# A scan's decays from cumulated rows, blocks of one chunk of all batches, and engine orders written by hand, in a kernel of SSD scan and hardswish MLP

## The chip, the cores and the metric

The kernel runs on one core of one Trainium2 chip. The metric is the device time of one execution in microseconds (us); the median of three runs is given. The core has TensorE (PE; its weight loads are listed apart as PEld), VectorE (DVE), ScalarE (ACT), GpSimd (POOL) and SyncE (SP), each with an instruction queue of its own, and 16 DMA engines. Transfers are issued here from SP's and ACT's queues.

## The reference

Two parts follow each other. The first is a scan (Mamba2 SSD) over 4 batches, 8 heads, 768 tokens, with 32 channels and 16 state rows per head; the second is an MLP with a hardswish between its two products, over 3072 tokens of 256 channels and 2048 inner channels.

```python
log_a = np.log(np.clip(a, 1e-06, 1.0))
for c in range(nc):                      # chunks of the sequence
    cum = np.cumsum(la, axis=-1)
    L = np.exp(cum[:, :, :, None] - cum[:, :, None, :]) * causal
    y_intra = einsum('bhij,bhjd->bhid', einsum('bhin,bhjn->bhij', Cc, Bc) * L, xc)
    y_inter = einsum('bhin,bhnd->bhid', Cc, state) * np.exp(cum)[:, :, :, None]
    y[:, :, sl] = y_intra + y_inter
    decay_from_j = np.exp(cum[:, :, -1:] - cum)
    state = exp(sum(la)) * state + sum_j(Bc * xc * decay_from_j)
x = y.transpose(0, 2, 1, 3).reshape(B * S, H * D)
h = x @ w_in
out = (h * np.clip(h + 3.0, 0.0, 6.0) / 6.0) @ w_out
```

The weights come as float64 and are made float32 on the chip; all products are float32. Both kernels take chunks of 128 tokens, which give the same sums as the reference's chunks of 32.

## The kernel before

`ssd(g)` does one chunk of one batch, so there are 24 of them. Decays between tokens come from PE: POOL spreads log a into `lu` (line 234), PE multiplies it by a triangle (`after`, line 242) and gets the sums of log a over (j, i] for all pairs of tokens, two heads at a time, in the first half of the PSUM tile `lg`. Beside it, in the other half, stands the product C.B of the same two heads (line 245), which uses 32 of PE's 128 rows. ACT takes the exponential (249), POOL sets what lies above the diagonal to zero (250), DVE multiplies the two halves into `M` (253). There are three `lg` buffers for the four pairs of heads. Then PE adds what the state gives (259) and the chunk's own part (265) in `y`, and the new state's product (275), and DVE scales and adds the state (278, 282). The chunk's C, B and scaled C are turned by PE (223).

A block of the MLP has 512 tokens: four chunks of one batch, or of two neighbouring ones. `mlp_in(k, f)` computes 128 of the 2048 inner channels (two matmuls, 295), ACT and DVE make the hardswish (299, 300: tiles `r` and `gT`); `mlp_out(k, t)` sums 16 matmuls for 128 tokens (306), ACT copies (310), SP stores (312). A weight piece (16 of them, 512 KB each) is loaded on ACT's queue (94) into one of three `raw` buffers and decoded by `decode_w` (110 to 126: five steps on DVE, three on POOL). The first block's four `ssd` and the eight pieces of `w_in` come ahead of the first `mlp_in`; the pieces of `w_out` and the next block's `ssd` are placed between the `mlp_in` and `mlp_out` of each block.

The order of instructions on each engine is made by the tile framework's scheduler, which ranks them by priority; it isn't the order of the program text. It sets the waits between engines too.

Of the kernel before, what the change touches and what calls it, by code (L numbers as in the profile page):

```python
# [12 lines left out]
PSUM = bass.MemoryType.PSUM  # L13


@with_exitstack
def kernel(
# [23 lines left out]
    NC = S // P                 # chunks in a sequence  # L41
    T = NB * S
    TB = 512                    # tokens in a block of the MLP
    NBLK = T // TB
    CPB = TB // P               # chunks in a block
# [4 lines left out]
    assert NH * N == P and NH * D == DM == 2 * P and D == 32 and 2 * N == 32  # L50
    assert DF == NF * P == 8 * PC and NC * P == S and NBLK * TB == T

    const = ctx.enter_context(tc.tile_pool(name="const", bufs=1))
    loads = ctx.enter_context(tc.tile_pool(name="loads", bufs=5))
    att = ctx.enter_context(tc.tile_pool(name="att", bufs=2))
    ffn = ctx.enter_context(tc.tile_pool(name="ffn", bufs=2))
    ps_l = ctx.enter_context(tc.tile_pool(name="ps_l", bufs=3, space=PSUM))
    ps_m = ctx.enter_context(tc.tile_pool(name="ps_m", bufs=1, space=PSUM))
    ps_y = ctx.enter_context(tc.tile_pool(name="ps_y", bufs=1, space=PSUM))
    ps_f = ctx.enter_context(tc.tile_pool(name="ps_f", bufs=3, space=PSUM))  # L60

# [1 line left out]
    moe_w_in, moe_w_out = moe_w_in.bitcast(U32), moe_w_out.bitcast(U32)  # L63
    a_sb = const.tile([NB * NH, S], FP32, name="a_sb")
# [4 lines left out]
    def load(g):  # L69
        b, c = divmod(g, NC)  # L70
        sl = slice(c * P, (c + 1) * P)
        bc = loads.tile([P, 2, NH, N], FP32, name="bc")
        xt = loads.tile([P, NH, D], FP32, name="xt")
        for j, src in enumerate((B, C)):
            nc.sync.dma_start(out=bc[:, j], in_=src[b, :, sl, :].rearrange("h s n -> s h n"))
        nc.sync.dma_start(out=xt, in_=x[b, :, sl, :].rearrange("h s d -> s h d"))
        loaded[g] = bc, xt

    for g in range(CPB):
        load(g)  # L80
# [3 lines left out]
    NP = 8                      # pieces of each weight matrix  # L84
    raws = {}

    def load_w(i):
        raw = loads.tile([P, 2, 2 * PC], U32, name="raw", bufs=3)
# [5 lines left out]
        nc.scalar.dma_start(out=raw, in_=src)  # L94
        raws[i] = raw

    def decode_w(i):
        """float64 words to float32: (1 + mantissa) * (sign, 2 ** exponent)."""
        words = raws.pop(i).rearrange("p k (f w) -> p k f w", w=2)
# [5 lines left out]
        e = att.tile([P, 2, PC], U32, name="we")  # L105
        m = att.tile([P, 2, PC], U32, name="wm")
        t = att.tile([P, 2, PC], FP32, name="wt")
        # the exponent, its bias changed from 1023 to 127, at float32's place;
        # what is too small for float32 becomes 0, what is too large infinite
        nc.vector.tensor_scalar(  # L110
# [16 lines left out]
        if i + 3 < 2 * NP:  # L127
            load_w(i + 3)

    for i in range(3):  # L130
        load_w(i)
# [67 lines left out]
    def ssd(g):  # L199
# [72 lines left out]
        if c == NC - 1:  # L272
            return
# [86 lines left out]
```

## Time and profile before

| | us |
|---|---|
| median of three runs | 551.46 |
| lowest and highest | 550.2 and 551.74 |
| span of the profiled execution | 548.1 |
| PE busy in it (90%) | 492.0 |
| DVE, POOL, ACT busy | 217.2, 125.3, 117.7 |
| matmuls of `mlp_in` (L295), busy | 174.4 |
| matmuls of `mlp_out` (L306), busy | 171.5 |
| matmuls of the decay sums (L242), busy | 59.0 |
| matmuls of the scores (L245), busy | 37.1 |

The profile is that of one execution; its times start with the span. Busy time of an engine is the union of its instructions; L242 is line 242 of the kernel. A group's line gives, after the bar, its busy time and the mean duration of one instruction, then the idle time of the engine ahead of these instructions and what ended most of it. Matmuls are pipelined and their ends are modelled, so what one costs in a row is read from start to start. In a row of a stretch, the numbers after the stretch and its length are the busy times of PE, PEld, DVE, ACT and POOL with their counts, then the granted clock of PE, the share of the DMA engines and GB/s.

### The profile page before, as it was taken

Reading aid. Unit: us, or ns where it says so; the run is one execution under the profiler, and the core shown is the slowest. Engines: PE = TensorE matmul, PEld = TensorE weight load, DVE = VectorE, ACT = ScalarE, POOL = GpSimd, SP = SyncE. Lnnn points to the kernel's source line nnn. Section 1 sums busy time; section 2 is a strip of 40 time slices with the busy share of each in tenths; the row PEclk is TensorE's granted clock in tenths of the full one; section 3 lists DMA queues with packets and bytes.
Section 4 is the critical chain, followed back from the end, with each engine's and each line's share of the span. In section 5 each row is a group of like instructions: output and inputs, shape, how many; then the busy total and the mean of one; then the engine's idle time right before and its main releaser. Section 6 shows DMA issues by size and latency. Waiting matters only on the chain.

```text
span 548.1 us, 5534 instructions
## 1 busy us (share of the span) xinstructions
PE 492.0 (90%) x2120; PEld 306.9 (56%) x2120; DVE 217.2 (40%) x404; ACT 117.7 (21%) x246; POOL 125.3 (23%) x178
## 2 busy tenths in 40 slices
PE   1697788899999898899898898999898999999997
PEld 1353333366754476663466664456674457774586
DVE  5978989732125522115522215422205452104300
ACT  1211033121032321122321122321112421114300
POOL 6574765612101202202202202012202021100000
PEclk9999899899999999999999999999999999999999
DMA  8834242111010101101101101101000000000000
GB/s 174 168 97 77 86 126 86 12 27 29 20 19 11 18 15 20 32 16 19 11 10 30 29 20 19 10 11 29 11 19 2 0 2 10 11 19 0 1 19 19
DMA packets 82761, 18.27 MB, mean 33 GB/s; under 512 B 75536, under 2 KB 78608, under 8 KB 82736
## 3 DMA queue, kind: packets, MB, share of 16 engines
q1 hardware_dynamic: 78384, 9.54, 11.7%
q10 hardware_dynamic: 4352, 8.39, 4.6%
q8 instruction: 16, 0.26, 0.2%
q14 instruction: 9, 0.07, 0.0%
HBM read 14.78 MB, written 3.15 MB: 33 GB/s over the span
## 4 chain that ended last, share of the span: by engine, by line
PE 69%; DVE 14%; POOL 10%; issue 4%; ACT 2%; DMA 1%; ACTq 0%; DVEq 0%
PE f L306 30%; PE f L295 25%; PE lg L242 6%; DVE M L253 4%; PE lg L245 4%; POOL L L250 3%; POOL lu L234 3%; DVE state L282 2%; PE y L265 2%; ACT L L249 2%; POOL we L113 2%; DVE we L117 1%; DMA raw<-in_moe_w_in_dram 1%; POOL we L115 1%; POOL wt L122 1%
## 5 line engine op out<-in xcount | busy, mean ns | idle before, releaser
L295 PE MATMUL f<-yT,w_in 128*128 128x512 f32 x384 | 174.4, 604 | 0.0
L306 PE MATMUL f<-w_out,gT 128*128 128x256 f32 x768 | 171.5, 381 | 0.0
L306 PEld LDWEIGHTS f<-w_out,gT 128*128 128x128 f32 x768 | 144.8, 190 | 24.4 <-issue 5.6
L300 DVE SCALAR_TENSOR_TENSOR gT<-r,f 128x512 f32<-128x512 f32 x96 | 65.8, 685 | 147.8 <-ACT r L299 147.1
L295 PEld LDWEIGHTS f<-yT,w_in 128*128 128x128 f32 x384 | 72.0, 192 | 82.9 <-issue 81.9
L250 POOL TENSOR_SCALAR_AFFINE_SELECT L<-L 128x256 f32<-128x256 f32 x96 | 40.7, 443 | 312.3 <-ACT L L249 311.9
L299 ACT ACTIVATE r<-f,half 128x512 f32<-128x512 f32 x96 | 66.0, 687 | 132.6 <-PE f L295 120.4
L242 PE MATMUL lg<-lu,after 128*128 128x256 f32 x192 | 59.0, 424 | 20.0 <-DVE M L253 17.2
L253 DVE TENSOR_TENSOR M<-L,lg 128x256 f32<-128x256 f32 x96 | 38.1, 418 | 67.7 <-POOL L L250 67.7
L242 PEld LDWEIGHTS lg<-lu,after 128*128 128x128 f32 x192 | 34.2, 202 | 34.4 <-DVE M L253 26.2
L249 ACT ACTIVATE L<-lg 128x256 f32<-128x256 f32 x96 | 32.0, 384 | 95.8 <-PE lg L245 92.9
L234 POOL TENSOR_TENSOR lu<-upto,la 128x1024 f32<-128x1024 f32 x24 | 47.2, 1968 | 10.0 <-PE lg L242 9.6
L310 ACT COPY ob<-f 128x256 f32<-128x256 f32 x24 | 8.9, 372 | 176.2 <-PE f L306 176.2
L265 PE MATMUL y<-M,xt 128*32 128x128 f32 x384 | 28.8, 292 | 16.3 <-DVE M L253 16.3
L245 PE MATMUL lg<-cT,bcT 32*128 32x256 f32 x192 | 37.1, 456 | 3.4 <-DVE cT L228 3.4
L265 PEld LDWEIGHTS y<-M,xt 128*32 128x32 f32 x384 | 11.6, 110 | 42.1 <-DVE M L253 26.7
L245 PEld LDWEIGHTS lg<-cT,bcT 32*128 32x128 f32 x192 | 15.8, 196 | 20.6 <-issue 9.2
L215 DVE TENSOR_TENSOR cs<-bc,e_to 128x128 f32<-128x128 f32 x20 | 5.9, 298 | 40.3 <-PE m L223 40.3
L282 DVE SCALAR_TENSOR_TENSOR state<-state,e_state 128x256 f32<-128x256 f32 x16 | 20.8, 1299 | 0.0
L228 DVE TENSOR_TENSOR cT<-m,parity 128x256 f32<-128x256 f32 x24 | 10.1, 419 | 25.6 <-ACT bcT L226 25.0
L113 POOL TENSOR_SCALAR we<-we 128x512 uint32<-128x512 uint32 x16 | 12.7, 791 | 17.3 <-DVE we L110 16.6
L275 PE MATMUL m<-xt,bs 128*128 128x256 f32 x40 | 15.0, 459 | 0.0
(50 smaller groups left out, 194.3 us busy)
## 6 DMA issues: line engine op xcount, KB each, us to landing
raw<-in_moe_w_in_dram ACTq DMA_DIRECT2D x8, 512.0 KB, 4.4
raw<-in_moe_w_out_dram ACTq DMA_DIRECT2D x8, 512.0 KB, 3.2
xt<-in_x_dram SPq DMA_DIRECT2D x24, 128.0 KB, 2.4
out_dram<-ob SPq DMA_DIRECT2D x24, 128.0 KB, 1.7
bc<-in_B_dram SPq DMA_DIRECT2D x24, 64.0 KB, 2.4
bc<-in_C_dram SPq DMA_DIRECT2D x24, 64.0 KB, 2.8
a_sb<-in_a_dram SPq DMA_DIRECT2D x1, 96.0 KB, 3.1
```

Of the source, the lines that this page charges most:

```text
L234: nc.gpsimd.tensor_tensor(out=lu, in0=upto.unsqueeze(1).to_broadcast([P, NH, P]), in1=la[:, c, b].unsqueeze(2).to_broadcast([P, NH, P]), o ...
L242: nc.tensor.matmul(out=lg[:, 0].rearrange("j h i -> j (h i)"), lhsT=after, rhs=lu[:, hs].rearrange("k h i -> k (h i)"), start=True, stop=True)
L245: nc.tensor.matmul(out=lg[:, 1].rearrange("j h i -> j (h i)"), lhsT=bcT[rows, 0], rhs=cT[rows].rearrange("n t i -> n (t i)"), start=True, ...
L249: nc.scalar.activation(L[:, hs], lg[:, 0], AF.Exp)
L250: nc.gpsimd.affine_select(out=L[:, hs], in_=L[:, hs], pattern=[[0, 2], [1, P]], compare_op=ALU.is_ge, fill=0.0, base=0, channel_multiplier=-1)
L253: nc.vector.tensor_tensor(out=M[:, hs], in0=L[:, hs], in1=lg[:, 1], op=ALU.mult)
L265: nc.tensor.matmul(out=y_ps[32 * q:32 * q + 32, t], lhsT=xt[:, h], rhs=M[:, h], start=(c == 0 and t == 0), stop=True, tile_position=(0, 32 ...
L282: nc.vector.scalar_tensor_tensor(out=new, in0=state[b], scalar=e_state[:, k:k + 1], in1=new, op0=ALU.mult, op1=ALU.add)
L295: nc.tensor.matmul(out=h, lhsT=w_in[:, j, f * P:(f + 1) * P], rhs=yT[:, j, k * TB:(k + 1) * TB], start=(j == 0), stop=(j == NK - 1))
L299: nc.scalar.activation(r, h, AF.Relu, bias=half, scale=1.0 / 6.0)
L300: nc.vector.scalar_tensor_tensor(out=gTs[k][:, f], in0=r, scalar=1.0, in1=h, op0=ALU.min, op1=ALU.mult)
L306: nc.tensor.matmul(out=o, lhsT=gTs[k][:, f, t * P:(t + 1) * P], rhs=w_out[:, f], start=(f == 0), stop=(f == NF - 1))
```

## The change

Decays: log a is cumulated once, heads on partitions, by a scan on DVE (`cum`), and stored in DRAM (`cum_d`). From there a row of all heads is broadcast to 128 partitions (`load_decay`, 512 KB each, 24 of them); POOL subtracts the sum at token j and sets what lies above the diagonal to -1e5, over 1024 elements at once; ACT takes the exponential. The products of PE for the sums are gone. `cum`'s rows are also broadcast for C's decay (`eto`, eight transfers a chunk).

Blocks: a block of the MLP is one chunk of all four batches, and a load brings a whole block's B, C or x (4096 pieces of 64 or 128 bytes each). B and C are turned two batches at a time (`turn`); C is scaled in the copy out of PSUM. The scores of four pairs of heads stand one after the other on PE, in four PSUM banks (`scores`). The state is kept as two halves of 64 rows (`mix`, `keep`). PSUM is one ring of six banks for h, o, cb and the transposes, and two banks for y.

Weights: decoding is split in two (`decode_a`, `decode_b`). DVE has four steps for a piece of `w_in` and three for one of `w_out`, ACT three and four, POOL one and two. Pieces are loaded on SP's queue, four buffers.

Order: `manual_schedule` keeps each engine's instructions in the order of the program text, which is written out at the end.

```diff
+    ctx.enter_context(tc.manual_schedule())
...
+    def big(shape, name):
+        return att.tile(shape, FP32, name=name, tag="big", bufs=5)
...
-        nc.scalar.dma_start(out=raw, in_=src)
+        nc.sync.dma_start(out=raw, in_=src)
...
+    def decode_a(i):
...
+        nc.vector.tensor_scalar(
+            out=e, in0=hi, scalar1=20, scalar2=0x7FF,
+            op0=ALU.logical_shift_right, op1=ALU.bitwise_and)
+        nc.scalar.activation(
+            e.bitcast(FP32), e, AF.Relu, bias=bias_hi, scale=-float(1 << 23))
+        nc.scalar.activation(e, e.bitcast(FP32), AF.Relu, bias=bias_lo, scale=-1.0)
+        nc.vector.tensor_scalar(
+            out=m, in0=hi, scalar1=0xFFFFF, scalar2=0x100000,
+            op0=ALU.bitwise_and, op1=ALU.bitwise_or)
+        mf = m.bitcast(FP32)
+        nc.scalar.activation(mf, m, AF.Copy, scale=2.0 ** -20)
+        if i < NP:
+            nc.vector.scalar_tensor_tensor(
+                out=mf, in0=lo, scalar=2.0 ** -52, in1=mf, op0=ALU.mult, op1=ALU.add)
+        else:
+            low = att.tile([P, 2, PC], FP32, name="wl", bufs=1)
+            nc.scalar.activation(low, lo, AF.Copy, scale=2.0 ** -52)
+            nc.gpsimd.tensor_tensor(out=mf, in0=low, in1=mf, op=ALU.add)
...
+    def decode_b(i):
...
         nc.vector.scalar_tensor_tensor(
             out=e, in0=hi, scalar=0x80000000, in1=e, op0=ALU.bitwise_and, op1=ALU.bitwise_or)
+        nc.gpsimd.tensor_tensor(
+            out=dst, in0=m.bitcast(FP32), in1=e.bitcast(FP32), op=ALU.mult)
+        if i + NRAW < 2 * NP:
+            load_w(i + NRAW)
...
+    nc.vector.tensor_tensor_scan(
+        out=flat, data0=run.rearrange("g c p -> g (c p)"), data1=a_sb, initial=0.0,
+        op0=ALU.mult, op1=ALU.add)
+    cum_d = dram.tile([NB, NC, NH, P], FP32, name="cum_d")
+    for b in range(NB):
+        nc.scalar.dma_start(
+            out=cum_d[b].rearrange("c h p -> h c p"), in_=cum[b * NH:(b + 1) * NH])
...
+    def load_decay(c, b, queue):
+        L = big([P, NH, P], "L")
+        src = cum_d[b, c].rearrange("h p -> (h p)").unsqueeze(0)
+        queue.dma_start(
+            out=L.rearrange("j h i -> j (h i)"), in_=src.to_broadcast([P, NH * P]))
+        Ls[c, b] = L
...
+    for b in range(NB):
+        load_decay(0, b, nc.scalar)
...
+    def decay(c, b):
+        L = Ls[c, b]
+        by_j = cum_t[:, c, b * NH:(b + 1) * NH].unsqueeze(2).to_broadcast([P, NH, P])
+        nc.gpsimd.tensor_tensor(out=L, in0=L, in1=by_j, op=ALU.subtract)
+        nc.gpsimd.affine_select(
+            out=L, in_=L, pattern=[[0, NH], [1, P]], compare_op=ALU.is_ge,
+            fill=-1e5, base=0, channel_multiplier=-1)
+        nc.scalar.activation(L, L, AF.Exp)
+
+    def ends(c):
+        bc, xt = loaded[c]
         if c < NC - 1:
...
+            nc.gpsimd.tensor_tensor(
+                out=bs, in0=bc[:, 1],
+                in1=e_from[:, c].unsqueeze(2).to_broadcast([P, NB * NH, N]), op=ALU.mult)
...
+        if c:
+            eto = etos[c]
+            nc.scalar.activation(eto, eto, AF.Exp)
+            if c < NC - 1:
...
+                nc.gpsimd.tensor_tensor(
+                    out=tmp, in0=states[c - 1],
+                    in1=eto[:, :, P - 1:P].to_broadcast([P, NB, P]), op=ALU.mult)
...
+    def turn(c, p):
...
+        for k in range(4):
+            j, b = k // 2, 2 * p + k % 2
+            nc.tensor.transpose(
+                out=t_ps[:, k],
+                in_=bc[:, j, b * NH:(b + 1) * NH].rearrange("s h n -> s (h n)"), identity=ident)
...
+        nc.scalar.copy(out=bT, in_=t_ps[:, 2:4])
...
+    def scores(c, b):
+        bT, cT, csT = bTs[c, b // 2]
+        cbs = []
+        for q in range(NQ):
+            rows = slice(32 * q, 32 * q + 32)
+            cb = ps.tile([P, 2, P], FP32, name="cb", tag="f")
+            nc.tensor.matmul(
+                out=cb.rearrange("j h i -> j (h i)"), lhsT=bT[rows, b % 2],
+                rhs=cT[rows, b % 2].rearrange("n t i -> n (t i)"), start=True, stop=True,
+                tile_position=(32 * q, 0))
+            cbs.append(cb)
+        L = Ls[c, b]
+        for q in range(NQ):
+            hs = slice(2 * q, 2 * q + 2)
+            nc.vector.tensor_tensor(out=L[:, hs], in0=L[:, hs], in1=cbs[q], op=ALU.mult)
...
+    decode_a(0)
+    turn(0, 0)
+    decode_a(1)
+    decode_b(0)
+    turn(0, 1)
+    ends(0)
+    for b in range(NB):
+        decay(0, b)
+        decode_a(b + 2)
+        decode_b(b + 1)
+    load(1)
+    for b in range(NB):
+        scores(0, b)
+        load_decay(1, b, nc.sync)
+        if b:
+            mix(0, b - 1)
+        if b == 2:
+            keep(0, 0)
+        if b < 2:
+            decode_a(b + 6)
+            decode_b(b + 5)
+        else:
+            decode_b(7) if b == 2 else None
+    mix(0, 3)
+    keep(0, 1)
+    load_eto(1)
+
+    def steps(c):
+        ends(c)
+        turn(c, 0)
+        decay(c, 0)
+        yield
+        turn(c, 1)
+        decay(c, 1)
+        yield
+        for b in range(NB):
+            scores(c, b)
+            if c + 1 < NC:
+                load_decay(c + 1, b, nc.sync)
+            if b + 2 < NB:
+                decay(c, b + 2)
+            if b:
+                mix(c, b - 1)
+            if b == 2:
+                keep(c, 0)
+            yield
+        mix(c, 3)
+        keep(c, 1)
+        if c + 1 < NC:
+            load_eto(c + 1)
+
+    todo = steps(1)
+    load(2)
+    for f in range(NF):
+        mlp_in(0, f)
+        if f % 2:
+            i = NP + f // 2
+            decode_a(i)
+            if i > NP:
+                decode_b(i - 1)
+        if f % 2 == 0 and f >= 2:
+            next(todo, None)
+    decode_b(2 * NP - 1)
+    for k in range(1, NC + 1):
+        if k < NC:
+            todo = steps(k + 1) if k + 1 < NC else iter(())
+            if k + 2 < NC:
+                load(k + 2)
+            for f in range(NF):
+                mlp_in(k, f)
+                if f in (9, 13):
+                    next(todo, None)
+        for b in range(NB):
+            next(todo, None)
+            if b < NB - 1:
+                mlp_out(k - 1, b, 0, NF)
+            else:
+                mlp_out(k - 1, b, 0, 12)
+                next(todo, None)
+                mlp_out(k - 1, b, 12, NF)
```

`mix(c, b)` is PE's part that follows on the scores: the state's product in two halves of 64 rows, eight products of `L` with x, and two products of 64 columns for the new state. `keep(c, p)` copies two batches of y into `yT` on ACT, and masks and adds the new state on DVE. `mlp_in` and `mlp_out` are as before but for the tiles they read, and `mlp_out(k - 1)` comes behind `mlp_in(k)`.

More of the change, by code (lines that the diff above doesn't have):

```diff
@@ new lines, in keep @@
+    def keep(c, p):
+        y_ps = y_pss[c]
+        if p == 0:
+            yTs[c] = att.tile([P, NK, NB, P], FP32, name="yT")
+            if c < NC - 1:
+                states[c] = att.tile([P, NB, P], FP32, name="state")
+        bs_ = slice(2 * p, 2 * p + 2)
+        for u in range(NK):
+            nc.scalar.copy(out=yTs[c][:, u, bs_], in_=y_ps[u][:, 0:2])
+        if c < NC - 1:
+            new = states[c][:, bs_]
+            nc.vector.tensor_tensor(
+                out=new, in0=y_ps[0][:, 2:4],
+                in1=mask.rearrange("p h d -> p (h d)").unsqueeze(1).to_broadcast([P, 2, P]),
+                op=ALU.mult)
+            if c:
+                nc.vector.tensor_tensor(out=new, in0=new, in1=tmps[c][:, bs_], op=ALU.add)
```

337 lines of the change are left out of this document (137 added, 200 removed).

## The prediction

> **What bounds the kernel now.** I read the page's busy line first, then busy time by stretches of the run, then PE's two stretches with nothing beside them.
>
> ```profile
> span 548.1 us, 5534 instructions
> PE 492.0 (90%) x2120; PEld 306.9 (56%) x2120; DVE 217.2 (40%) x404; ACT 117.7 (21%) x246; POOL 125.3 (23%) x178
> ```
>
> ```profile
> 0.00:64.00 64.00, 39.76 (x179) 21.42 (x180) 49.62 (x86) 10.68 (x26) 39.48 (x56) 0.96 0.58 119
> 64.00:112.00 48.00, 41.00 (x140) 18.50 (x139) 41.23 (x77) 13.67 (x26) 27.40 (x34) 0.95 0.31 80
> ...
> 140.00:225.00 85.00, 79.17 (x356) 50.47 (x356) 28.33 (x55) 18.93 (x40) 13.88 (x20) 1.00 0.13 19
> ```
>
> ```profile
> 489.90:517.40 27.50, 27.50 (x66) 12.19 (x65) 10.31 (x15) 10.68 (x16) 0.00 (x0) 1.00 0.02 5
> 517.40:545.10 27.70, 27.62 (x128) 23.96 (x127) 0.69 (x1) 1.80 (x5) 0.00 (x0) 1.00 0.04 14
> ```
>
> The columns of the lower two are the stretch, its length, then PE, PEld, DVE, ACT, POOL. The rows of 27.5 and 27.7 us are one block of the MLP with nothing beside it: 27.5 us in, 27.6 us out, 55.1 us. A block that carries four `ssd` beside it takes 85 us (third stretch), so four `ssd` cost 30 us, 24 of them PE's own work and 6 idle. The middle is bound by PE. The first 112 us are bound by the way there, with PE, DVE and POOL all half to four fifths busy: until 64 us the first block's `ssd` and the decoding of `w_in`, until 112 us the decoding of `w_out`. Six bare blocks are 331 us; all the rest is what a change can win.
>
> **The middle: what PE no longer does.** PE's scan work is read where one `ssd` stands in a row:
>
> ```profile
> 203.05 0.38 PE L223 MATMUL m<-ident,bc 128*128 128x128 f32 x2
> ...
> 204.77 0.71 PE L245 MATMUL lg<-cT,bcT 32*128 32x256 f32 x6
> ...
> 205.41 0.71 PE L259 MATMUL y<-bcT,state 128*128 128x128 f32 x4
> ...
> 207.56 0.69 PE L245 MATMUL lg<-cT,bcT 32*128 32x256 f32 x2
> ...
> 208.18 0.63 PE L265 MATMUL y<-M,xt 128*32 128x128 f32 x12
> ...
> 208.74 0.70 PE L275 MATMUL m<-xt,bs 128*128 128x256 f32 x2
> ```
>
> A float32 product is two instructions. From start to start, three scores (x6) take 0.64 us and one (x2) 0.62: products in different rows of the array already run together, and a group costs mostly its start. So the four scores of a `scores`, now with nothing between them, take 0.65 us, at most 4/3 of 0.64. `mix` has three groups: the state's product (at most its present 0.54), eight `L` products (x12 took 0.56, so 0.7 for x16) and the new state (at most the present 0.54; I take 0.5). A `turn` is eight transposes in a chunk at 0.11 us and two starts, 1.1 us. A chunk of four batches: 4 × (0.65 + 0.54 + 0.7 + 0.5) + 1.1 = 10.7 us, against 24. The four chunks 2 to 5 that stand beside the MLP after its first block cost 41 us (the last makes no state). Gone are the sums of log a (L242, 1024 columns each `ssd`), a third of the transposes, and PE's wait for a freed `lg`: `scores` and `mix` now stand a whole `mlp_out` (6.9 us) apart.
>
> What may wait there instead is ACT. At f = 9 it must do `eto`, then POOL's `tmp`, subtraction and selection follow, then `Exp`, about 6 us with `r` queued behind it. PE runs on through its six `ps` banks (five h, 8.6 us), so I cost this at 1.3 us a block, 5 in all, and 6 a block if that cover is gone.
>
> **The way there: what an order by hand adds.** Each engine now keeps the program's order. I follow the first stages through the queues with these rows:
>
> ```profile
> L299 ACT ACTIVATE r<-f,half 128x512 f32<-128x512 f32 x96 | 66.0, 687 | 132.6 <-PE f L295 120.4 <-DMA raw<-in_moe_w_out_dram 8.7 <-DVE cs L215 2.1
> L300 DVE SCALAR_TENSOR_TENSOR gT<-r,f 128x512 f32<-128x512 f32 x96 | 65.8, 685 | 147.8 <-ACT r L299 147.1
> ...
> L234 POOL TENSOR_TENSOR lu<-upto,la 128x1024 f32<-128x1024 f32 x24 | 47.2, 1968 | 10.0 <-PE lg L242 9.6
> L250 POOL TENSOR_SCALAR_AFFINE_SELECT L<-L 128x256 f32<-128x256 f32 x96 | 40.7, 443 | 312.3 <-ACT L L249 311.9
> L253 DVE TENSOR_TENSOR M<-L,lg 128x256 f32<-128x256 f32 x96 | 38.1, 418 | 67.7 <-POOL L L250 67.7
> ...
> L249 ACT ACTIVATE L<-lg 128x256 f32<-128x256 f32 x96 | 32.0, 384 | 95.8 <-PE lg L245 92.9 <-DVE wt L124 2.8
> ```
>
> ```profile
> 5.56 0.43 DVE L110 TENSOR_SCALAR we<-raw 128x512 uint32<-128x512 uint32 x1 [4.21 <-DMA raw<-in_moe_w_in_dram]
> 5.90 0.42 DVE L120 TENSOR_SCALAR wm<-raw 128x512 uint32<-128x512 uint32 x1
> 6.08 0.72 POOL L113 TENSOR_SCALAR we<-we 128x512 uint32<-128x512 uint32 x1 [3.81 <-DVE we L110]
> ```
>
> After the bar of the upper rows stand the busy time and the mean ns of one. Estimates from them: the subtraction 1.97 us, as `lu`; the selection of 1024 elements between 0.44 (L250's whole time, if size cost nothing) and four times that, 1.77, and I take 1.4, nearer to the upper end since the other rows grow with size; `Exp` of 1024 from L249 and L299 (256 more elements, 0.3 us more) at most 1.37, twice `r`, and I take 1.1; an activation of a weight piece 0.69 as `r`; DVE's two-input steps 0.69 as `gT`; POOL's product of 512 half of `lu`, 0.98; a hand-over 0.09 (DVE ends 5.99, POOL starts 6.08).
>
> In `for b: decay(0, b); decode_a(b + 2); decode_b(b + 1)` these stand in a ring. POOL's subtraction and selection of b wait behind its product of piece b; `Exp` waits for them; the three activations of piece b + 2 are queued behind `Exp`; DVE's sum needs the third; DVE's sign step of piece b + 1 is queued behind that sum; POOL's product needs it, and the next subtraction is queued behind the product. One turn: 1.97 + 1.4 + 1.1 + 3 × 0.69 + 0.69 + 0.69 + 0.98 + 6 × 0.09 = 9.4 us, with each engine idle most of it.
>
> When it starts is set by the DMA:
>
> ```profile
> q1 hardware_dynamic: 78384, 9.54, 11.7%
> ...
> raw<-in_moe_w_in_dram ACTq DMA_DIRECT2D x8, 512.0 KB, 4.4
> ...
> bc<-in_C_dram SPq DMA_DIRECT2D x24, 64.0 KB, 2.8
> ```
>
> The raws go from ACT's queue to SP's, behind `load(0)`: 12288 of those 78384 packets, 0.157 × 11.7% × 548 = 10 us of all engines. The first piece lands at about 15 us, the others with the four broadcasts between them. The scan of log a, its four stores and the broadcasts' issue on ACT hold ACT's decoding back to 14 us; the raws hide that, and if they were early it would be late next. Then two pieces' `decode_a` (0.43 + 2.07 + 0.2 + 0.69 = 3.4 each), `cT` 0.7, the sign step 0.69, a product and `bs` 0.98 each: POOL's first subtraction at 25. Four turns end with the fifth sign step at 25 + 4 × 9.4 − 1.1 = 61.5. Behind it stand 16 products by the scores (6.7), `decode_a` of two pieces (6.8), three sign steps (2.1), the state and the last `mix` with its two copies (2.4): the first `mlp_in` starts at **79.5 us**, against 64.24 before:
>
> ```profile
> 64.24 7.79 PE L295 MATMUL f<-yT,w_in 128*128 128x512 f32 x16
> ```
>
> In the first block the same ring has another shape. Two f with a `decay` between: POOL's sum 0.98, its product 0.98, subtraction and selection 3.37, `Exp` 1.1, `r` 0.69, `gT` 0.69, DVE's exponent 0.43, four activations 2.75, hand-overs 0.6: 11.6 us, with 4.9 us of work for PE (two h, 3.4, and one batch's share of the scan). The start (two h, `r`, `gT`, exponent, four activations) 8.5; the pair with `ends` 12.6 (`tmp` more); three pairs 11.6; then two without decay, 6.3 and 7.2; `yT` at f = 14 after 1.6: 71 us, so the second block's `mlp_in` starts at **150.5**. Since `mlp_out(0)` comes after it, 5 × 27.5 + 6 × 27.6 of MLP remain, 303; with 41 of scan and 5 of waits PE ends at 499.5.
>
> ```profile
> 545.10 0.37 ACT L310 COPY ob<-f 128x256 f32<-128x256 f32 x1 [6.58 <-PE f L306]
> ```
>
> The tail from PE's end, just before this copy, to 548.1 stays 3.1: a span of 502.6. The median of the runs (551.46) stands 3.4 above the profiled span; I add that: **506 us**. So the middle gives 16 to 18 us in each of four blocks and the way there takes back some 20.
>
> **The clock.** PE is idle for about 6 us in each of those turns.
>
> ```profile
> 20.00:24.00 4.00, 0.58 (x5) 0.31 (x6) 4.00 (x8) 0.27 (x1) 1.95 (x3) 1.00 0.98 211
> ...
> 52.00:56.00 4.00, 4.00 (x16) 2.41 (x16) 2.03 (x6) 0.94 (x3) 1.32 (x3) 0.57 0.30 42
> ```
>
> The third number from the right is the granted clock: 1.00 while PE was nearly idle, 0.57 later for a few us at full work, so the trace shows dips but not a rule. The Trainium skill (TensorE: Matmul & The Clock Gate, Part 1) says that PE falls to half its clock after an idle window of about 3.4 us and needs as long a busy one to come back; the 20 to 24 row doesn't agree. As a mechanism of this kernel: PE's 38 us of work from 79.5 to 150.5 at half clock are 76, 5 more than the ring gives, 511 us in all.
>
> **Rivals.** *The rings don't close* (if an engine runs ahead of the order I read, or POOL and ACT are quicker on these shapes): then the busiest engine bounds each stage, DVE with 30 us of work (eight pieces at 2.24, sixteen products at 0.42, some 5 of others) after 15 for the start, ACT with 40 (16 `r`, 32 activations, the rest 7) in the first block: 85 + 303 + 41 + 5 + 3.1 + 3.4 = 440. For it: no engine in those stages is over 60% busy by my sum. Against: in-order queues, and the ring has no slack in it. *Waits in the middle too*: 6 us in each of four blocks and 2-us DVE steps in the turns, about 535. *The broadcasts bind*, the slower side: 24 loads of 512 KB queue on one DMA ring, and each hands its `L` to a turn. A raw piece of that size landed in 4.4 us; a 64-KB load of small packets in 2.8, and eight of those would be 22. If a broadcast takes longer than a turn it replaces it: 4 × (t − 9.4) + 4 × (t − 11.6) + 16 × (t − 17) for the middle's quarter blocks of 17 us. The gain of 45 us is gone at t = 16; at 22 the sum is 172 us, 678 in all. Against it: the rows of a broadcast are 4 KB, like raw's 2 KB and unlike the 64 bytes of `bc`. That the scan's sums don't fall away at all can't be: they are not in the program.
>
> **How the numbers follow.** Forecast 0.58: 506, its own range 488 to 530 (the eight turns by −1.0 to +0.7 us each, the selection and `Exp` at their ends, the start by 5 either way, the middle's waits from 0 to 15). Half clock 0.05: 511. Rings open 0.20: 440, reaching to 480. Waits in the middle 0.06: 535. Broadcasts bind 0.08: above 551. No change 0.03. About 0.3% is what a measurement of this kernel can tell from no change. Faster by more than that: 0.58 + 0.05 + 0.20 + 0.06 = 0.89; within it 0.03; slower 0.08. The range: above 540 lie 0.11, and half of the open rings may lie below 450, 0.10: 450 to 540.
>
> **What would show it.** Right: the first `mlp_in` at 75 to 85 us, POOL, ACT and DVE each below half busy there, ACT's activations waiting for `Exp` and `Exp` for the selection; the second block's `mlp_in` at 140 to 155; then blocks of 66 to 68 us with PE busy over 95%. Wrong: `mlp_in` at 50; blocks of 72 or more, with PE waiting for `gT` or a bank; a subtraction waiting for a DMA; scores that take 0.6 us each and not all four.

## The result, and the profile after

The changed kernel takes **489.2 us** (median of 4 runs, 488.88 to 489.56), the kernel before, on the same chip, 550.83 us (549.77 to 551.74): a ratio of 0.888, 95% interval 0.886 to 0.890. Forecast were 506 us and a range of 450 to 540. The head of the page of the changed kernel, its busy line and PE's row of the slices:

```profile
span 487.4 us, 5024 instructions
PE 411.1 (84%) x1948; PEld 258.6 (53%) x1948; DVE 158.4 (33%) x300; ACT 147.6 (30%) x245; POOL 112.6 (23%) x90
...
PE   2200189457799999999999999999999999999997
```

PE's busy time fell from 492 to 411 us, 81 us, and the span by 61. The PE row tells both halves of the story: from the 12th slice on (each is 12 us) PE is hardly ever idle; ahead of that lie five slices with next to no work for PE and, in the first block, four at 4 to 7 tenths. The same in windows (stretch, length, PE, PEld, DVE, ACT, POOL, granted clock, DMA share, GB/s), first the wait ahead of the first `mlp_in`, then the first block, then the second, which the later ones resemble:

```profile
15.00:60.00 45.00, 3.82 (x14) 2.21 (x16) 23.25 (x27) 17.01 (x26) 19.12 (x14) 1.00 0.29 104
75.10:142.80 67.70, 49.24 (x200) 20.51 (x200) 26.46 (x58) 33.02 (x55) 28.31 (x22) 0.82 0.45 118
142.80:207.90 65.10, 65.09 (x328) 41.70 (x329) 24.26 (x48) 20.73 (x36) 20.41 (x16) 1.00 0.23 55
```

A block in the middle takes 65.0 us in place of 85, all of it PE. From 15 to 60 us no engine is busy for more than 52% of the time (DVE, 23 of 45 us): none is full there, and each waits for about half of the time or more. The first `mlp_in` starts at 75.1 us (64.2 before), the first block's `mlp_in` ends at 142.8 (at 111.7 before, where chunk 1's scan lay behind it). So the way there costs 31 us more, and from there to the end of PE it is 341.5 us in place of 433.4, 92 less. The difference is the 61 us.

The waits of the changed kernel (engine, waiting tile, what released it: us in total, times, the longest):

```profile
POOL w_in L168 <- DVE we L166: 46.7, 8, 20.4
...
ACT L L238 <- POOL L L235: 55.5, 11, 6.7
...
PE cb L289 <- DVE L L297: 36.3, 3, 34.6
...
POOL L L234 <- DMA L<-cum_d: 19.0, 3, 6.9
...
PE cb L289 <- DVE gT L363: 6.7, 2, 3.5
```

POOL waits for DVE, ACT for POOL, PE for DVE: the sign of a ring. It is read from one turn of `for b: decay(0, b); decode_a(b + 2); decode_b(b + 1)` in the timeline (start, duration, engine, instruction; in brackets the idle time before it and what ended it):

```profile
34.19 1.90 POOL L234 TENSOR_TENSOR L<-L,cum_t 128x1024 f32<-128x1024 f32 x1
34.27 2.10 DVE L139 TENSOR_SCALAR we<-raw 128x512 uint32<-128x512 uint32 x1 [1.38 <-POOL w_in L168]
36.16 1.16 POOL L235 TENSOR_SCALAR_AFFINE_SELECT L<-L 128x1024 f32<-128x1024 f32 x1
36.29 1.31 DVE L145 TENSOR_SCALAR wm<-raw 128x512 uint32<-128x512 uint32 x1
37.35 1.06 ACT L238 ACTIVATE L<-L 128x1024 f32<-128x1024 f32 x1 [5.79 <-POOL L L235]
38.31 0.71 ACT L142 ACTIVATE we<-we,bias_hi 128x512 f32<-128x512 uint32 x1
39.05 0.72 ACT L144 ACTIVATE we<-we,bias_lo 128x512 uint32<-128x512 f32 x1
39.68 0.61 ACT L149 ACTIVATE wm<-wm 128x512 f32<-128x512 uint32 x1
40.33 0.69 DVE L151 SCALAR_TENSOR_TENSOR wm<-raw,wm 128x512 f32<-128x512 uint32 x1 [2.73 <-ACT wm L149]
40.93 0.69 DVE L166 SCALAR_TENSOR_TENSOR we<-raw,we 128x512 uint32<-128x512 uint32 x1
41.70 1.26 POOL L168 TENSOR_TENSOR w_in<-wm,we 128x512 f32<-128x512 f32 x1 [4.39 <-DVE we L166]
42.92 1.89 POOL L234 TENSOR_TENSOR L<-L,cum_t 128x1024 f32<-128x1024 f32 x1
```

Read by its start times, the column is a baton: POOL subtracts and selects, ACT takes `Exp` and then three activations, DVE its two steps, POOL its product, and only then the next subtraction. 42.92 − 34.19 = 8.7 us a turn, in which each engine works 3 to 5 us. The first block's ring is the same with `r` and `gT` in it; its subtractions start at 98.67 and 109.57, 10.9 us apart.

### The profile page after: what moved, and what is told of

Same layout as the page of the kernel before. It is cut to its first block, busy times and chain, and to the rows that moved or that the text cites. A ratio compares the mean times of both kernels' runs of the same rounds, so it can differ in the third digit from the quotient of the medians.

```text
span 487.4 us, 5024 instructions
## 1 busy us (share of the span) xinstructions
PE 411.1 (84%) x1948; PEld 258.6 (53%) x1948; DVE 158.4 (33%) x300; ACT 147.6 (30%) x245; POOL 112.6 (23%) x90
## 3 DMA queue, kind: packets, MB, share of 16 engines
q1 hardware_dynamic: 87952, 29.73, 25.3%
## 4 chain that ended last, share of the span: by engine, by line
PE 71%; issue 12%; POOL 8%; ACT 4%; DMA 3%; DVE 2%; POOLq 0%; DVEq 0%; ACTq 0%; SPq 0%
PE o L371 35%; PE h L357 28%; POOL L L234 3%; PE cb L289 2%; DMA L<-cum_d 2%; PE y L318 2%; POOL L L235 2%; PE y L312 1%; POOL w_in L168 1%; PE y L324 1%; ACT we L144 1%; ACT we L142 1%; POOL wm L156 1%; POOL w_out L168 1%; PE t_ps L267 1%
## 5 line engine op out<-in xcount | busy, mean ns | idle before, releaser
L357 PE MATMUL h<-yT,w_in 128*128 128x512 f32 x384 | 177.5, 616 | 12.2 <-DVE gT L363 10.8
L371 PE MATMUL o<-w_out,gT 128*128 128x256 f32 x768 | 171.3, 382 | 0.0
L371 PEld LDWEIGHTS o<-w_out,gT 128*128 128x128 f32 x768 | 144.3, 190 | 23.4 <-issue 4.1
L357 PEld LDWEIGHTS h<-yT,w_in 128*128 128x128 f32 x384 | 73.7, 197 | 103.5 <-issue 80.5
L363 DVE SCALAR_TENSOR_TENSOR gT<-r,h 128x512 f32<-128x512 f32 x96 | 64.9, 686 | 131.4 <-ACT r L362 131.0
L362 ACT ACTIVATE r<-h,half 128x512 f32<-128x512 f32 x96 | 64.5, 685 | 65.5 <-PE h L357 65.5
L289 PE MATMUL cb<-cT,bT 32*128 32x256 f32 x192 | 27.5, 478 | 54.6 <-DVE L L297 36.3
L297 DVE TENSOR_TENSOR L<-L,cb 128x256 f32<-128x256 f32 x96 | 33.9, 416 | 79.4 <-PE cb L289 79.4
L234 POOL TENSOR_TENSOR L<-L,cum_t 128x1024 f32<-128x1024 f32 x24 | 45.7, 1903 | 19.0 <-DMA L<-cum_d 19.0
L235 POOL TENSOR_SCALAR_AFFINE_SELECT L<-L 128x1024 f32<-128x1024 f32 x24 | 26.5, 1102 | 1.8
L156 POOL TENSOR_TENSOR wm<-wl,wm 128x512 f32<-128x512 f32 x8 | 10.2, 1270 | 45.1 <-ACT wl L155 45.1
L318 PE MATMUL y<-L,xt 128*32 128x128 f32 x384 | 17.2, 302 | 0.0
```

Source lines behind the costliest of these rows:

```text
L234: nc.gpsimd.tensor_tensor(out=L, in0=L, in1=by_j, op=ALU.subtract)
L235: nc.gpsimd.affine_select(out=L, in_=L, pattern=[[0, NH], [1, P]], compare_op=ALU.is_ge, fill=-1e5, base=0, channel_multiplier=-1)
L289: nc.tensor.matmul(out=cb.rearrange("j h i -> j (h i)"), lhsT=bT[rows, b % 2], rhs=cT[rows, b % 2].rearrange("n t i -> n (t i)"), start=Tr ...
L297: nc.vector.tensor_tensor(out=L[:, hs], in0=L[:, hs], in1=cbs[q], op=ALU.mult)
L318: nc.tensor.matmul(out=y_ps[u][32 * q:32 * q + 32, k], lhsT=xt[:, b * NH + h], rhs=L[:, h], start=(c == 0), stop=True, tile_position=(0, 3 ...
L357: nc.tensor.matmul(out=h, lhsT=w_in[:, j, f * P:(f + 1) * P], rhs=yTs[k][:, j].rearrange("p b i -> p (b i)"), start=(j == 0), stop=(j == N ...
```

## The experiments

Each time below is the median; the ratio is to the kernel before. "First `mlp_in`" is the end of the start, "first block" the time from there to the second block's `mlp_in`. In the edits `decay` is cut in two: `decay_pool` (subtraction and selection) and `exp_of` (ACT's `Exp`).

| kernel | us | ratio (95%) | first `mlp_in` | first block | a block after |
|---|---|---|---|---|---|
| changed | 489.2 | 0.888 (0.886–0.890) | 75.1 | 67.7 | 65.0 |
| `Exp` behind, start | 480.6 | 0.874 (0.870–0.878) | 65.8 | 68.2 | 65.0 |
| `Exp` behind, first block | 475.1 | 0.864 (0.860–0.868) | 75.3 | 53.5 | 65.0 |
| three buffers | 489.6 | 0.889 (0.887–0.891) | 75.4 | 67.4 | 65.0 |
| `Exp` behind in both, three buffers | 462.4 | 0.840 (0.838–0.842) | 61.9 | 54.5 | 65.0 |
| the same, product on DVE | 464.6 | 0.843 (0.840–0.846) | 65.3 | 51.9 | 65.0 |
| no order by hand | 463.0 | 0.842 (0.840–0.844) | 64.9 | 52.1 | 65.0 |
| no order by hand, all three edits | 459.8 | 0.834 (0.832–0.836) | 62.5 | 52.1 | 65.0 |
| selection twice | 504.1 | 0.917 (0.912–0.921) | 80.1 | 73.5 | 66.4 |
| broadcasts twice | 501.2 | 0.911 (0.909–0.914) | 74.9 | 79.5 | 65.0 |
| four banks | 518.0 | 0.942 (0.938–0.946) | 75.5 | 80.1 | 69.1 |
| sums behind the scores | 518.3 | 0.943 (0.938–0.947) | 75.2 | 66.9 | 72.5 |
| sums between the scores | 580.6 | 1.056 (1.048–1.063) | 89.3 | 69.9 | 82.4 to 86.8 |

### Are the first 143 us bound by rings?

If so, one link taken out of the ring shortens every turn, though no engine gets less work. In the start `Exp` is issued behind the next piece's activations:

```
     for b in range(NB):
-        decay(0, b)
+        decay_pool(0, b)
         decode_a(b + 2)
+        exp_of(0, b)
         decode_b(b + 1)
```

> One edit: in the loop of the start, Exp of batch b is issued behind the activations of weight piece b + 2, not ahead of them; nothing else moves. Theory (the ring POOL product, subtraction, selection, Exp, activations, DVE sum, sign step sets the start): the ring now spans two batches, so a batch costs 4.5 to 5.5 us in place of 8.7, the first mlp_in starts at 58 to 63 us in place of 75.1, and all behind it keeps its length: 472 to 478 us. Rival (the landing of the weights or DVE's own work sets the start): mlp_in stays within 2 us of 75, total within 2 of 489.

It came out at 480.6 us, 8.6 less, and the whole of it lies ahead of the first `mlp_in` (65.8 for 75.1). The ring is shown, but a turn fell to 6.84 us (POOL's subtractions at 37.47 and 44.31), 1.9 less and not 3 or 4, so the total stands above the expected 472 to 478. The timeline on DVE names what is late next:

```profile
37.55 2.10 DVE L139 TENSOR_SCALAR we<-raw 128x512 uint32<-128x512 uint32 x1 [1.38 <-POOL w_in L168]
```

DVE's exponent step of piece b + 2 is released by POOL's product of piece b, which frees the `we` buffer (there are two). So it starts just when POOL begins its subtraction, and takes 2.10 us in place of 0.42. A second ring, through a buffer, stood behind the one through the queues.

The same in the first block, where chunk 1's `Exp` goes behind the activations of the next `w_out` piece:

```
             i = NP + f // 2
             decode_a(i)
+            while late:
+                exp_of(*late.pop())
             if i > NP:
```

> One edit: in the first block of the MLP, the Exp of chunk 1's decays is issued behind the next weight piece's activations. Start as it is (75.1). Theory: ACT no longer waits for POOL, so a pair of inner tiles takes 6 to 7 us in place of 10.9, the first block 46 to 52 us in place of 67.7, second mlp_in at 122 to 127, total 469 to 474. Rival (PE at the halved clock of this stretch, or the chain over ACT and DVE within a pair, bounds it anyway): first block over 60 us, total over 481.

475.1 us, 14.1 less, all of it in the first block: 53.5 us for 67.7. It lies 1.5 us above the expected stretch of 46 to 52, and the window says why:

```profile
75.30:128.90 53.60, 44.24 (x201) 18.96 (x201) 31.80 (x58) 32.71 (x55) 28.66 (x22) 0.87 0.60 152
```

With the ring open PE is busy 44 of 53.6 us, at a granted clock of 0.87: close to being the bound.

Then the buffers, alone and with both edits:

```
-        e = att.tile([P, 2, PC], U32, name="we")
-        m = att.tile([P, 2, PC], U32, name="wm")
+        e = att.tile([P, 2, PC], U32, name="we", bufs=3)
+        m = att.tile([P, 2, PC], U32, name="wm", bufs=3)
```

> The kernel after with three buffers for the exponent and mantissa words of a weight piece in place of two; orders as they are. Theory: in the ring of the kernel after, DVE's exponent step waits for the buffer that POOL's product frees, but has several us to spare before the ring's Exp is done, so nothing changes: 487 to 491 us, mlp_in at 74 to 76. Rival (the two buffers were a second lock of the start all along): mlp_in below 72, total below 486.

> Both rings opened (Exp behind the next activations in the start and in the first block), and three buffers for the words. Theory: with Exp alone moved, a batch of the start fell to 6.8 us, not to 5, since DVE's exponent step then waited for POOL's product to free its buffer and ran into POOL's subtraction (2.10 us in place of 0.42). With a third buffer it is issued earlier: 4.5 to 5.5 us a batch, mlp_in at 58 to 62; the first block 50 to 54 as with its own ring open; total 457 to 464. Rival (POOL's and DVE's common work holds it at 6.8): mlp_in at 65 to 67, total 465 to 468.

Both came as expected: the third buffer alone gives nothing (489.6), since the queue's ring is the longer one; with the `Exp` edits in place the total is 462.4, and a turn of the start 5.54 us. The two edits alone gave 8.6 and 14.1, together 22.7; the 26.8 here are 4.1 more, so the buffer is worth about 4 us once the first ring is open. One turn's DVE and POOL there:

```profile
31.01 2.07 POOL L234 TENSOR_TENSOR L<-L,cum_t 128x1024 f32<-128x1024 f32 x1
...
32.05 1.58 DVE L151 SCALAR_TENSOR_TENSOR wm<-raw,wm 128x512 f32<-128x512 uint32 x1 [0.72 <-ACT wm L149]
...
33.56 1.57 DVE L166 SCALAR_TENSOR_TENSOR we<-raw,we 128x512 uint32<-128x512 uint32 x1
```

Two engines are now nearly full in the turn: POOL's subtraction, selection and product take 2.07, 1.43 and 1.38 of its 5.54 us, and DVE's two steps shown here, now beside POOL's, take more than twice the 0.69 they had alone. To relieve POOL, its product for `w_in` was moved to DVE:

```
-        nc.gpsimd.tensor_tensor(
+        (nc.vector if i < NP else nc.gpsimd).tensor_tensor(
```

> As the run with both rings open and three buffers, and the last product of the w_in pieces done by DVE in place of POOL. Theory: POOL keeps 3.0 us a batch, DVE has 2.9 of its own and fewer waits for POOL: mlp_in at 54 to 60, total 453 to 462. Rival (DVE is full by then): no better than the run without it.

It missed: 464.6 us (462.64 to 465.93), no gain. The start is 3.4 us later and the first block 2.6 shorter; the work that POOL lost stands on DVE instead, the fullest engine of the start.

Is it the order by hand that closes the rings, and not the new operations? One line is taken out, so that the planner sets the order, as it did before the change:

```
-    ctx.enter_context(tc.manual_schedule())
```

> The kernel after without its one line that keeps the program's order; the scheduler orders each engine by priority. Theory: PE's work in the middle is the same, so a block stays at 65 to 70 us; the two rings are made by the order, so a scheduler that sees their idle engines opens them in part: mlp_in at 55 to 75, total 465 to 495. Rival (the order by hand is what gives the middle its 100% of PE): blocks of 72 or more, total 510 to 540.

463.0 us, 2 under the expected 465 to 495: **the order by hand costs 26 us**, 10.2 in the start and 15.6 in the first block, and the middle does not need it (65.0 both ways). POOL's timeline shows what the planner does with the same instructions:

```profile
19.44 2.05 POOL L233 TENSOR_TENSOR L<-L,cum_t 128x1024 f32<-128x1024 f32 x1 [16.94 <-DMA L<-cum_d]
21.56 1.43 POOL L234 TENSOR_SCALAR_AFFINE_SELECT L<-L 128x1024 f32<-128x1024 f32 x1
...
27.01 3.75 POOL L233 TENSOR_TENSOR L<-L,cum_t 128x1024 f32<-128x1024 f32 x2
```

It lets the subtractions and selections run ahead of the products, and decodes later; nobody hands a baton. Taken together with the edits above:

> The same kernel, without the line that keeps the program's order. Theory: the scheduler gave 463.0 with the rings in the program; with them open in the program too it finds less to gain: within 8 us of the run by hand, either way, blocks of 65.0 in both.

459.8 us (458.33 to 461.2, 4 runs), ratio 0.834: the best version, 29 us under the changed kernel and 91 under the one before. Its windows, the start and the first block:

```profile
15.00:62.50 47.50, 19.55 (x112) 8.68 (x112) 40.49 (x59) 24.97 (x40) 26.03 (x16) 1.00 0.79 207
62.50:114.60 52.10, 45.13 (x200) 19.73 (x201) 39.91 (x62) 36.34 (x61) 41.33 (x30) 0.90 0.56 134
```

Now work, not waiting, fills both: DVE is busy 40.5 of 47.5 us in the start, PE 45 of 52 in the first block.

### What the single terms are worth

The selection issued twice (the second leaves the values as they are) prices one of the ring's terms:

```
+        nc.gpsimd.affine_select(
+            out=L, in_=L, pattern=[[0, NH], [1, P]], compare_op=ALU.is_ge,
+            fill=-1e5, base=0, channel_multiplier=-1)
```

> The selection is issued twice in a row on the same tile (the second changes nothing): 1.1 us more of POOL for each of 24 decays. Theory: in the ring eight times, each at full price, so mlp_in at 75.1 + 4.4, the first block 67.7 + 4.4, the four blocks behind unchanged at 65.0: 498 us. If POOL is hidden in the first stages: 489. If POOL binds in the middle too: 1.1 x 24 = 26 more, 515.

504.1 us, 14.9 more where 9 were expected. The start took 5.0 of them and the first block 5.8, four selections of 1.10 us and a little more, as a ring must. The 1.4 us in each later block were not expected. PE's timeline in the second block, at the end of `mlp_in`:

```profile
182.16 1.36 PE L292 MATMUL cb<-cT,bT 32*128 32x256 f32 x8
184.33 5.85 PE L374 MATMUL o<-w_out,gT 128*128 128x256 f32 x26 [0.80 <-DVE gT L366]
```

From the first batch's scores to the `o` behind them it is 2.17 us, where the changed kernel takes 0.64 (scores at 171.35, `o` at 171.99): that is 1.5, all that the block lost. The longer POOL stage puts `Exp` later, `r` and `gT` behind it are late, and PE stands for `gT` at the end of the stage. In the changed kernel that cover is just about used up.

How much the cover is worth is seen with four banks in place of six:

```
-    ps = ctx.enter_context(tc.tile_pool(name="ps", bufs=6, space=PSUM))
+    ps = ctx.enter_context(tc.tile_pool(name="ps", bufs=4, space=PSUM))
```

> The PSUM ring of h, o, cb and the transposes with four banks in place of six. Theory (ACT waits some 4 to 5 us for POOL at f = 9 of each block and PE runs on through free banks): with four, three h (5.2 us) cover it just about, and the scores need all four banks at once, so PE waits there for the last products of the hardswish: 2 to 5 us a block, blocks of 67 to 70. The start has no h and stays; the first block, in which the ring is tight already, may lose up to 15. Total 495 to 525. Rival (the cover is not needed): blocks 65, total within 3 of 489.

518.0 us, as expected: 4.1 us more in each block, 12.4 in the first. One of its waits, to be held against the same line of the changed kernel above, and PE at the end of `mlp_in` and behind an `mlp_out`:

```profile
PE cb L289 <- DVE gT L363: 20.4, 10, 4.5
```

```profile
185.15 0.71 PE L289 MATMUL cb<-cT,bT 32*128 32x256 f32 x6
186.72 0.69 PE L289 MATMUL cb<-cT,bT 32*128 32x256 f32 x2 [0.86 <-DVE gT L363]
187.34 5.01 PE L371 MATMUL o<-w_out,gT 128*128 128x256 f32 x22
...
194.45 1.23 PE L289 MATMUL cb<-cT,bT 32*128 32x256 f32 x8
195.60 0.49 PE L312 MATMUL y<-csT,state 64*128 64x128 f32 x4
```

Ten waits of 20.4 us in all, where there were two of 6.7: the fourth score stands until `gT` has freed a bank. Six of them, 17.0 us, lie in the first block; each later block has one, of 0.86, which is only part of its 4.1. At the end of `mlp_in` the scores take 2.19 us (185.15 to 187.34) and not 0.64, 1.5 more, and a transpose waits 0.5 ahead of it; behind an `mlp_out` they take 1.15 (194.45 to 195.60), 0.5 more in each of three batches. The total was hit, but a lost cover for `Exp` is about 2 us a block and not the 6 of the prediction; another 1.5 is scores that no longer all stand together, and some 0.6 is not accounted for.

Do the broadcasts bind? Those of chunks 1 to 5 are loaded twice, the second over the first:

```
+        for _ in range(2 if c else 1):
             queue.dma_start(
```

> Each broadcast of the decays of chunks 1 to 5 is loaded twice into the same tile (20 loads of 512 KB more). Theory: the landings stand ahead of POOL's need by more than their own time, or POOL's wait for them is off the path: total within 3 us of 489, blocks 65. Rival (broadcasts bind): each adds 2 to 6 us to the stage that it feeds, 40 to 100 us in all.

This missed: 501.2 us, 12 more. The blocks stayed at 65.0; all of it is in the first block. The wait that is new:

```profile
ACT eto L253 <- DMA eto<-cum_d: 11.6, 1, 11.6
```

The second load of a pair writes where the first does and waits on SP's queue until that has landed, some 5.9 us (in SP's rows of the timeline), and chunk 1's `eto` is queued behind them; it lands late, and ACT's queue stands behind `eto`. So this run doubles the bytes and adds a wait on SP's queue; the middle has room for both, SP's queue at the first block has none for the wait. It does not tell what the bytes alone would do there.

Last, the middle. Is its gain the sums of log a that PE no longer does, or does their place among the scores count as well? Four products of the size of those sums (all 128 rows by 256 columns) are added to each batch, into a part of the banks that nobody reads: once behind the four scores, once one behind each score.

```
+        for cb in cbs:
+            nc.tensor.matmul(
+                out=cb[:, 1].rearrange("j h i -> j (h i)"), lhsT=ident,
+                rhs=xt[:, 0:8].rearrange("s h d -> s (h d)"), start=True, stop=True)
```

> The kernel after, with PE given back work of the size of the removed decay sums: four products of 128x128 by 256 columns behind the four scores of each batch, into the unused half of their banks; nobody reads them. Theory (PE alone bounds the middle, the rings the first two stages): 1.7 to 1.9 us for each batch, so a block of 65.0 becomes 72 to 73, the first two stages move by under 3 us, total 517 to 521. Rival (the gain of the middle came from waits, not from PE's work): blocks under 68, total under 502.

> The same added products as in the run with the sums behind the scores, but one of them between every two scores, as the kernel before had them. Theory (four scores in different rows run together only when nothing stands between them, and each change between 32 and 128 rows costs a start): each score costs 0.62 alone in place of 0.65 for four, and each sum its own start, 2.4 us more for each batch than with the sums behind: blocks of 80 to 83 us, total 550 to 560, about that of the kernel before. Rival (the order of the products does not matter): as with the sums behind, blocks of 72 to 73, 517 to 521.

Behind: 72.5 us a block, as expected, 7.5 more for 16 products, 0.47 each. Between: 82.4 us in the second block, 17.4 more for the same 16 products. The timelines of the scan of one batch, of the changed kernel:

```profile
179.10 0.71 PE L289 MATMUL cb<-cT,bT 32*128 32x256 f32 x8
179.74 0.49 PE L312 MATMUL y<-csT,state 64*128 64x128 f32 x4
180.16 0.64 PE L318 MATMUL y<-L,xt 128*32 128x128 f32 x16
180.74 0.44 PE L324 MATMUL y<-xt,bs 128*64 128x128 f32 x4
181.11 1.13 PE L371 MATMUL o<-w_out,gT 128*128 128x256 f32 x4
```

and of the kernel with the sums between:

```profile
271.25 0.69 PE L290 MATMUL cb<-cT,bT 32*128 32x256 f32 x2
271.87 0.70 PE L295 MATMUL cb<-xt,ident 128*128 128x256 f32 x2
```

Four scores with nothing between them take 0.64 us (179.10 to 179.74); a score alone takes 0.62 (271.25 to 271.87). With the sums between, 16 scores and 16 sums at 0.62 are 19.8 us where four groups of scores had been 2.6: 17.2, against 17.4 measured. So the same 16 products cost 7.5 us a block behind the scores and 17.4 between them: their place alone is worth 9.9 (82.4 − 72.5). The total of 580.6 us is above the expected 550 to 560: the start came 14 us later, and the third and fourth block took 86.8 and 85.3 (below).

That place is not the one that the sums had in the kernel before, though its program text alternates them with the scores. Its planner put three sums together and then three scores, and only the fourth of each stood alone. Around the scores at 204.77 and 207.56 that the prediction shows, the kernel before has these sums:

```profile
203.38 1.46 PE L242 MATMUL lg<-lu,after 128*128 128x256 f32 x6
...
206.93 0.70 PE L242 MATMUL lg<-lu,after 128*128 128x256 f32 x2 [0.81 <-DVE M L253]
```

So the 9.9 us are no part of the 20 us that a block lost; they are what that order costs in the changed kernel, and show what the planner had already avoided. By the start times of the four `ssd` in the 85-us block, the sums took 7.9 us (7.5 when put back behind the scores), and the scores 5.0, where they now take 2.6. PE stood idle for 5.8 (85.00 − 79.17), mostly for `M` as in the last row, where it now hardly stands at all (65.10 − 65.09). The remaining 3.9 us are smaller groups, such as transposes and parts of y that stood alone; no run takes them apart. The gain of the middle is then above all the sums that are gone, with the waits that went with them second, and only 2.4 us are scores that now all stand together.

## Why the prediction was right, and where its sizes were off

The total is 16.8 us below the forecast, well inside its range, and its steps take that apart:

| step | predicted | measured | difference |
|---|---|---|---|
| first `mlp_in` | 79.5 | 75.1 | −4.4 |
| first block | 71 | 67.7 | −3.3 |
| from there to PE's end | 349 | 341.5 | −7.5 |
| median less PE's end | 6.5 | 4.9 | −1.6 |

Of the signs named beforehand two lie just outside: DVE is busy for 52% of the start, not below half, and a block takes 65.0 us, not 66 to 68.

**The start** went as written: rings, in the order of engines that the prediction gives, with the first subtraction at 25.3 us (25). The turn was 8.7 us, not 9.4, and most of the difference is the six hand-overs of 0.09, which are not there. The durations of the nine instructions of a turn add up to 8.80 us (1.90 + 1.16 + 1.06 + 0.71 + 0.72 + 0.61 + 0.69 + 0.69 + 1.26) and the turn takes 8.73, since in one queue an instruction starts some 0.1 us before the one ahead of it ends (38.31 above, where `Exp` ends at 38.41). The selection took 1.16 us where 1.4 was chosen; POOL's product took 0.28 more than the 0.98 put down for it, though two other products of 512 elements on POOL (`bs`, `tmp`) took 1.05. Four turns make 2.8 of the 4.4 us. **The first block** was a ring of 10.9 us a pair rather than 11.6: no hand-overs of 0.6 either, and a selection of 1.09, while POOL's two products of 1.27 each took back nearly 0.6. That `Exp` in ACT's queue closes both is shown by the two `Exp` runs, and that the order by hand does so by the run without it.

**The middle** is bound by PE, as said. The 41 us for the scans of four chunks are 38.5 (341.5 − 303). A chunk that makes a state takes 9.9 (65.0 less the bare 55.1) rather than 10.7: by the start times above a batch takes 0.64 + 0.42 + 0.58 + 0.37 = 2.0 us, where the terms taken were 0.65 + 0.54 + 0.7 + 0.5 = 2.4. The state products were held at their price from before, where each stood among others. And the 5 us of waits at f = 9 did not come. The timeline there:

```profile
160.51 7.03 PE L357 MATMUL h<-yT,w_in 128*128 128x512 f32 x16
...
165.66 1.06 ACT L238 ACTIVATE L<-L 128x1024 f32<-128x1024 f32 x1 [3.91 <-POOL L L235]
166.62 2.40 ACT L362 ACTIVATE r<-h,half 128x512 f32<-128x512 f32 x4
...
167.38 0.60 PE L267 MATMUL t_ps<-ident,bc 128*128 128x128 f32 x4
```

ACT did wait, and four `r` stood queued behind `Exp`, but PE went from `h` to `t_ps` without a gap. The cover was named rightly; the price set beside it (1.3 us a block) stands for a cover that holds only in part, and here it held.

**The rivals.** That the rings stay open (440) did not happen in this kernel, and the reason against it (in-order queues with no slack) is what the runs show. Opened by hand or by the planner they gave 459.8 to 463.0, not 440: that sum let DVE and ACT work at their own pace, with 85 us for the start and the first block together, but DVE's steps grow beside POOL's, and the two stages take 114.6 us in the best run; what else holds them was not taken apart. A loss in the middle came only with a longer POOL stage (1.4 us a block) or four banks (4.1), never the 6 of that rival. The broadcasts don't bind: they land in 5.8 us (the median of SP's; ACT's four in 7.8), inside a turn. POOL did stand for one three times, 19.0 us in the waits above, and the prediction named such a wait as a sign of being wrong. All three lie in the fourth block, where POOL has run ahead to the last chunk's tiles, and that block takes 65.0 us like the others, so they are off the path. **The clock** did fall, to a mean of 0.82 in the first block, and for a stretch further:

```profile
90.00:105.00 15.00, 3.83 (x8) 1.78 (x8) 5.16 (x11) 7.12 (x11) 6.27 (x5) 0.65 0.27 61
```

PE does 4 us of work in those 15 and is no member of the ring, so a slower pace costs nothing while the ring sets the time, and the 5 us of that rival did not come. The Trainium skill (TensorE: Matmul & The Clock Gate, Part 1) says that PE falls to half its clock after a short idle window; in the first block the trace agrees, with 0.65 granted where PE stands idle for 3.2 to 4.5 us at a time. The prediction read 1.00 in an idle stretch before as speaking against that rule. That reading can't be relied on, as the last section shows.

## What to carry to other kernels

Where the program's order is kept on several in-order engines, write down one turn of each loop as a baton (who waits for whom, and what is queued behind the waiting instruction) before any busy share is read: a ring costs the sum of its members, here 8.7 and 10.9 us a turn, with each engine at work for about half of it or less. Open a ring at the instruction that nobody in it needs (here `Exp`), and look at once for the next one, which may run through a buffer instead of a queue. Products in different rows of PE's array are cheap only while they stand together (here 0.64 us for four, 0.62 for one alone), so keep products of another shape out from between them.

## What was not expected of the hardware

**DVE's steps beside POOL.** A step of 0.42 us took 2.10 beside POOL's subtraction (34.27 above; it ends 0.28 us after the subtraction does) and 1.31 beside its selection; two-input steps went from 0.69 to 1.58. The Trainium skill (SBUF — State Buffer, Who interferes with whom) says that the two share a pair of ports, that a DVE step in a two-port mode or with two inputs in SBUF needs it, and that it is locked for one of them at a time. These rows agree; in which mode the one-input steps ran, no run here shows.

**PE's pace while the clock column says 1.00.** The first scores of the changed kernel, after 34.6 us with PE idle:

```profile
59.47 1.54 PE L289 MATMUL cb<-cT,bT 32*128 32x256 f32 x4 [34.63 <-DVE L L297]
60.94 1.08 PE L318 MATMUL y<-L,xt 128*32 128x128 f32 x16
61.95 0.70 PE L324 MATMUL y<-xt,bs 128*64 128x128 f32 x4
```

The 16 products `y<-L,xt` take 1.01 us from start to start, against 0.58 at 180.16, though the column gives 1.00 for the stretch from 51 to 61 us and for that from 61 to 75.1. So the pace of PE after a long idle stretch is read from the durations, not from that column. In the second stretch PE is busy for 12.0 of 14.1 us, so its pace may well lengthen the end of the start; the prediction counted no slow PE there. Nor did a busy stretch bring the pace back: with the sums between, PE had no gap from 59.3 to 88.8 us and each score or sum still took 1.15 us, against 0.62 later; the 12 `h` from 89.25 on ran at 0.44 us each, full pace. The Trainium skill (TensorE: Matmul & The Clock Gate, Part 1) has half a clock after an idle window, which fits these durations (1.7 to 1.9 times the later ones), and full clock again after a busy window as long, which does not. That it is the clock that slows these products is not shown, since the column says otherwise.

**A lower clock with PE always busy.** The third block of the kernel with the sums between:

```profile
241.60:328.40 86.80, 86.80 (x362) 51.98 (x361) 21.03 (x40) 18.20 (x31) 13.92 (x10) 0.94 0.21 46
```

PE is busy all the time; the clock is granted at 0.94, and the block is 4.4 us longer than the second, which had 1.00. The same products behind the scores ran at 1.00 in their second and third block. What lowers the clock there was not tried and stays open; so does what would bring the start below 62 us.
